# A re-planned order of loads, stores and matmuls in a fused attention and adapter kernel

## The chip, the cores and the metric

The kernel runs on one core of one Trainium2 chip. A core has a matrix engine (PE), a vector engine (DVE), a scalar engine (ACT), a general engine (POOL) that here only issues loads, and a sync engine (SP) that here only issues stores. Sixteen DMA engines move data between the main memory and the on-chip memory (SBUF). PE writes its results to eight banks of a second memory (PSUM). The metric is the device time of one execution in microseconds (us); lower is better. A profile of one execution has a span that is a little shorter than that time.

## The reference

For each of four batches, with N = 6400 rows and C = 256 channels, a 256 x 256 attention matrix is made from k and q, summed over the rows; then it is applied to v. On every row of that result a small mixture of eight adapters is added, of which the two with the largest gates count.

```python
qn = q / (norm(q, axis=1) + 1e-06)          # B, N, C = 4, 6400, 256, fp32
kn = k / (norm(k, axis=1) + 1e-06)
s = kn.transpose(0, 2, 1) @ qn / tau        # 256 x 256 for each batch
a = softmax(s)
x = (v @ a).reshape(B * N, C)               # 25600 x 256
logits = x @ w_gate                         # 8 experts
topk = two largest logits of each row; w = softmax over those two
delta = sum over the two: w * ((x @ A[e]) @ B[e])   # rank 16
return x + delta
```

So q, k and v are read once (3 x 26.2 MB) and the output is written once (26.2 MB). All of q and k of a batch must have arrived before any output row of that batch can be made.

## The kernel before

The kernel is a Python program that first plans and then emits. A small event simulation (`Plan.run`) plays all steps on five engines and a DMA model, and the order in which it starts them becomes the order of the instructions on each engine. Rows are split over 128 partitions; a batch has 50 "columns" of 128 rows. Loads of q and k come in three parts per batch (17, 17, 16 columns), v in five blocks of ten columns, and so does the output.

```python
STORE = {"zl": 1, "bank": 6, "qk": 6, "v": 3, "vT": 4, "y": 7, "gate": 3, "gz": 4, "gzT": 4, "sq": 1, "ssq": 2, "port": 1}
```

These are the numbers of buffers: three for v blocks, four for transposed v blocks, seven for output blocks. The steps that matter:

```python
def do_load(s, what, b, i, c, n):           # POOL issues; fp32 in memory becomes bf16 in SBUF
    if what == "v":
        t, src, c0 = sb(s, "v", (b, i), [P, PC * max(n for _, n in V), C], BF16), v_v, c
    ...
    nc.gpsimd.dma_start(t[:, c - c0:c - c0 + n, :], src[b, :, c:c + n, :])

def do_G(s, b, c):                          # k.T q of one column, and with it k.T k and q.T q
    for ic in range(CC):
        nc.tensor.matmul(acc[ic][:, 0:256], kt[:, j, ic::CC], qt[:, j, :], ...)
    for ic in range(0 if (b, group_of(c), "k") in OFF else CC):
        nc.tensor.matmul(acc[ic][:, 256:384], ...)      # norm of k on PE
    for ic in range(0 if (b, group_of(c), "q") in OFF else CC):
        nc.tensor.matmul(acc[ic][:, 384:512], ...)      # norm of q on PE
```

For the groups of columns in `OFF` the norms are not made on PE: ACT squares the columns (`do_sq`) and DVE adds the squares (`do_add`, `do_red`). After the last G of a batch comes a chain of short steps (`accs`, `n2`, `rsqrt`, `rq_ps`, `s`, `exp`, `aT`, `waA`, `a`) that makes the attention matrix. Each v block then goes through: `T` (transpose on PE), `Te` (copy out), then for a block in `MERGED` `ZL` (gate logits and adapter input in one matmul) and `ZLe`, or for another block `log` and later `Z`; the gates `m1` to `g2` on DVE; `Ze`, `gzT`, `gzTe`; `Y` (v times a, plus the adapter's output) and `Ye`, the copy to the output buffer by ACT or DVE.

```python
def do_Ye(s, b, i, c):
    copy(s, sb(s, "y", (b, i), [P, PC, C], FP32)[:, c:c + 2, :], held["bank", ("Y", b, i, c)])

def do_store(s, b, i, c, n):                # SP issues
    lo = i * PC + c
    nc.sync.dma_start(out_v[b, :, lo:lo + n, :], held["y", (b, i), ""][:, c:c + n, :])
```

A store can be held back until a given load has landed (`HOLD`). This is done by a small copy in SP's queue that reads the end of that load's tile; the store follows it:

```python
def do_hold(s, kind, b, i):
    src = ...                               # 16 elements of the last column of that load
    nc.sync.dma_start(scrap, src)
```

The planner's DMA model serves the load queue and the store queue in proportion to a size of packet, with fixed latencies:

```python
LAT = 0.07
DMA_LAT = 1.8
ISSUE = 0.55
ISSUE_LAT = 1.8
STORE_LAT = 1.4
...
WORDS = ('q10 v00 v01 v02 q11 v03 q12 v04 v10 v11 q20 v12 v13 v14 q21 v20 v21 v22 q22 q30 '
         'q31 q32 v23 v24 v30 v31 v32 v33 v34')       # order of loads after q and k of batch 0
HOLD = {(0, 0): ('k', 3, 1), (0, 1): ('k', 1, 2), (0, 4): ('k', 3, 2), (1, 0): ('k', 3, 1),
        (1, 1): ('k', 3, 2), (1, 2): ('k', 3, 2), (1, 3): ('k', 3, 2), (1, 4): ('k', 3, 2),
        (2, 0): ('k', 3, 1), (2, 1): ('k', 3, 2), (2, 4): ('k', 3, 1)}
```

A word such as q11 stands for part 1 of q and of k of batch 1; v03 is block 3 of v of batch 0. `do_warm` fills idle time of PE with matmuls whose result is not used, so that PE's clock stays up.

Of the kernel before, what the change touches and what calls it, by code (L numbers as in the profile page):

```python
# [18 lines left out]
class Step:  # L19
# [3 lines left out]
    def __init__(self, key, eng, deps, rank, take, give, size=0.0):  # L23
        self.packet = max(size, 0.08)
        self.key, self.eng, self.deps, self.rank = key, eng, deps, rank
        self.take, self.give, self.size = take, give, size
        self.users, self.place = [], {}
        self.ready, self.end, self.on = 0.0, None, None
        self.left = len(deps)
        self.only = next(iter(eng)) if len(eng) == 1 else None  # L30


class Clock:


    WINDOW, FIRST, LOW, HIGH = 3.413, 0.31, 0.5, 0.8
# [32 lines left out]
class Plan:  # L69

    LAT = 0.07
    DMA_LAT = 1.8
    ENGINES = ("PE", "DVE", "ACT", "POOL", "SP")
    ISSUE = 0.55
    ISSUE_LAT = 1.8
    STORE_LAT = 1.4
    OUT = 8

# [15 lines left out]

    def run(self, head):
# [4 lines left out]
        loads, queue, stores = list(self.loads), [], []  # L100
        now, out, left = 0.0, 0, sum(s.key[0] != "warm" for s in self.steps.values())
        free["POOL"] = 0.2
        clock = Clock()

# [5 lines left out]
        def can_take(s):  # L110
            return all((kind, name) in held or self.store[kind] for kind, name in s.take)

        def start(s, eng):
            for kind, name in s.take:
                if (kind, name) not in held:
                    held[kind, name] = self.store[kind].pop(0)
                    s.place[kind] = held[kind, name]
            s.on = eng
            s.t = now
            self.out.append(s)  # L120

# [5 lines left out]
        while left:  # L127
            again = False
            if (loads and free["POOL"] <= now + 1e-9 and out < self.OUT and can_take(loads[0])):
                s = loads.pop(0)  # L130
                start(s, "POOL")
                out += 1
                free["POOL"] = now + self.ISSUE
                push(free["POOL"], "free", None)
                push(now + self.ISSUE_LAT, "asked", s)
                again = True
            for e in self.ENGINES:
# [3 lines left out]
                for s in wait[e]:  # L141
                    if not can_take(s) or (s.key[0] == "warm" and not clock.idle(now)):
                        continue
# [3 lines left out]
                    if best is None or (s.rank, s.seq) < (best.rank, best.seq):  # L147
                        best = s
# [7 lines left out]
                if e == "SP":  # L156
                    push(now + self.STORE_LAT, "store", best)
                else:
                    push(free[e], "end", best)
# [3 lines left out]
            busy = [x for x in (queue, stores) if x]  # L163
            t = events[0][0] if events else float("inf")
            base = max(now, head)

            share = sum(x[0].packet for x in busy)
            if busy:
                t = min(t, base + min(x[0].size / x[0].packet for x in busy) * share)
            assert t < float("inf"), [s.key for s in self.steps.values() if s.end is None][:20]  # L170
            if t > base:
                for x in busy:
                    x[0].size -= (t - base) * x[0].packet / share
                    if x[0].size < 1e-6:
                        push(t + self.DMA_LAT, "landed", x[0])
                        out -= x is queue
                        x.pop(0)
            now = max(now, t)
            while events and events[0][0] <= now + 1e-9:
                _, _, what, s = heapq.heappop(events)  # L180
                if what == "asked":
                    queue.append(s)
                elif what == "store":
                    stores.append(s)
# [3 lines left out]
                elif what == "landed":  # L188
                    push(now + (SAFE if s.on == "POOL" else 0.0), "end", s)
                    for u in s.users:  # L190
                        if u.key[0] == "hold":
                            u.left -= 1
                            if u.left == 0:
                                push(now, "ready", u)
                elif what == "end":
# [6 lines left out]
                    for u in s.users:  # L202
                        u.left -= u.key[0] != "hold"
                        if u.left == 0 and u.eng and u.key[0] != "hold":
                            push(now + (0.0 if s.on == u.only else self.LAT), "ready", u)
# [10 lines left out]
V = ((0, 1), (1, 1), (2, 1), (3, 1), (4, 1))  # L216
# [13 lines left out]

def make_plan(B, order, ahead):
# [6 lines left out]
    for kind, b, i in order:  # L238
        if kind == "v":
            p.add(("load", "v", b, i, V[i][0] * PC, V[i][1] * PC), {}, (), 0, take=(("v", (b, i)),),  # L240
                  size=LOAD * V[i][1] * PC + 0.062)
            continue
        for c, n in PARTS.get((b, i), QK[i:i + 1]):
            for h in "qk":
                p.add(("load", h, b, i, c, n), {}, (), 0, take=(("qk", (h, b, i)),), size=LOAD * n + 0.062)

    for h in "qk":
        p.add(("cast", h), {"ACT": 0.6}, [("load", h, 0, 0) + PARTS[0, 0][0]], 0)
    p.loads[2].size += 0.5
    for b in range(B):  # L250

        for i, (c0, n) in enumerate(QK):
            for c in range(c0, c0 + n):
# [8 lines left out]
                p.add(("G", b, c), {"PE": 0.442 - 0.112 * sum((b, group_of(c), w) in OFF for w in "kq")}, deps,  # L262
# [4 lines left out]
        for w in "kq":  # L267
# [5 lines left out]
            for x, g in enumerate(halves):  # L273
                c, n = GROUPS[g]
                i = max(i for i, q in enumerate(QK) if q[0] <= c)
                p.add(("sq", w, b, g), {"ACT": 0.2 + 0.2125 * n},
                      [k for k in p.steps if k[:4] == ("load", w, b, i) and k[4] < c + n and c < k[4] + k[5]]
                      + [("cast", w)] * ((b, c) == (0, 0)), pos["qk", b, i] - SQ, take=(("ssq", (w, b)) if x == 0 else ("sq", (w, b, g)),),
                      give=(("qk", (w, b, i)),))
                if x:  # L280
                    p.add(("add", w, b, g), {"DVE": 0.15 + 0.268 * n},
# [4 lines left out]
            if halves:  # L286
                p.add(("red", w, b), {"DVE": 1.9}, [before], pos["qk", b, len(QK) - 1] - 1, give=(("ssq", (w, b)),))
                p.add(("n2p", w, b), {"PE": 0.35}, [("red", w, b), ("G", b, NC - 3)], -100, take=(("bank", ("n2p", w, b)),))
                late.append(w)
        if b == 0:  # L290
            p.add(("wts",), {"DVE": 1.8}, [("load", "k", 0, len(QK) - 1) + PARTS[0, len(QK) - 1][1]], -200)
# [3 lines left out]
        p.add(("accs", b, 1), {"ACT": 0.38}, [end], ch)  # L295
        p.add(("n2", b, 0), {"DVE": 0.45}, [end], ch)
        p.add(("accs", b, 0), {"ACT": 0.38}, [("n2", b, 0)], ch)
        p.add(("n2", b, 1), {"DVE": 0.45}, [("accs", b, 1)], ch)
        p.add(("rsqrt", b), {"DVE": 1.9 + 0.2 * len(late)},
              [("n2", b, 0), ("n2", b, 1)] + [("n2p", w, b) for w in late], ch, take=(("port", b),),  # L300
              give=(("port", b),) + tuple(("bank", ("n2p", w, b)) for w in late))
        p.add(("rq_ps", b), {"PE": 0.45}, [("rsqrt", b)], ch, take=(("bank", ("rq", b)),))
        for ic in range(2):
            p.add(("s", b, ic), {"DVE": 0.42}, [("rq_ps", b), ("accs", b, ic)], ch, give=(("bank", ("rq", b)),))
            p.add(("exp", b, ic), {"ACT": 0.68}, [("s", b, ic)], ch)
            p.add(("aT_ps", b, ic), {"PE": 0.14}, [("exp", b, ic)], ch, take=(("bank", ("aT", b)),))
        p.add(("recip", b), {"DVE": 0.17}, [("exp", b, 0), ("exp", b, 1)], ch)
        p.add(("aT", b), {"DVE": 0.42}, [("aT_ps", b, 0), ("aT_ps", b, 1)], ch, give=(("bank", ("aT", b)),))
        p.add(("waA_ps", b), {"PE": 0.35}, [("aT", b), ("wts",)], ch, take=(("bank", ("waA", b)),))
        p.add(("waA", b, 0), {"DVE": 0.35}, [("waA_ps", b), ("recip", b)], ch, give=(("bank", ("waA", b)),))  # L310
# [676 lines left out]
```

## Time and profile before

| what | value |
|---|---|
| device time, median of 3 runs | 254.41 us (254.39 to 254.47) |
| span of the profiled execution | 252.7 us (its device time 254.46) |
| PE busy | 217.8 us, 86% of the span |
| DVE busy | 192.7 us, 76% |
| ACT busy | 151.1 us, 60% |
| mean granted clock of PE | 0.986 of full speed |
| read from and written to main memory | 78.91 MB, 26.21 MB |

The page lists busy time by engine, then the span in 40 slices with one digit each (9 means 90% or more), the DMA queues (q0 carries the loads that POOL issues, q1 what SP issues, q10 what ACT issues), the chain of work that ended last, and the costliest groups of instructions. A group line has the line of the kernel, the engine and the operation, the output and the input with their shapes, the count, the busy time, the mean of one in ns, and the idle time of that engine just before, with what ended it. In the table of stretches, the DMA share is the mean busy share of the sixteen DMA engines; it can be a little above 1 since packets overlap. GB/s there counts the bytes that arrive.

### The profile page before, as it was taken

How to read it: one execution, taken by the hardware profiler on the slowest of the kernel's cores; microseconds unless marked ns; L12 is line 12 of the kernel's file. 1: busy time of each engine (PE TensorE's matmuls, PEld its weight loads, DVE VectorE, ACT ScalarE, POOL GpSimd, SP SyncE). 2: the span in 40 equal slices, each digit the busy share in tenths (PEclk: the TensorE clock that was granted, in tenths of full speed). 3: DMA queues.
4: the chain of work that ended last, by engine and by line, in shares of the span. 5: the costliest groups of instructions: out<-in, count | busy, mean ns of one | idle time of the engine just before them, and what ended most of it. 6: DMA issues, size and time to landing. Idle time of an engine off the chain costs nothing.

```text
span 252.7 us, 5852 instructions
## 1 busy us (share of the span) xinstructions
PE 217.8 (86%) x2357; PEld 193.0 (76%) x2357; DVE 192.7 (76%) x528; ACT 151.1 (60%) x269; POOL 27.1 (11%) x54
## 2 busy tenths in 40 slices
PE   0274995988999998689999999889999979999990
PEld 0162882876999996579899899779999769999980
DVE  0055589869899987588899899489898898889850
ACT  5454427546786543975667768362674846657671
POOL 7003010040002002000500100500000000000000
PEclk9998899999999999999999999999999999999997
DMA  8999999999999999999999999999999999999996
GB/s 251 217 217 209 211 223 208 217 218 215 215 217 241 303 305 298 224 213 221 210 215 220 215 217 217 211 212 313 317 251 353 322 341 317 337 392 415 404 408 249
DMA packets 11243, 66.70 MB, mean 264 GB/s; under 512 B 1360, under 2 KB 1744, under 8 KB 6608
## 3 DMA queue, kind: packets, MB, share of 16 engines
q0 software_dynamic: 6912, 38.80, 74.4%
q1 hardware_dynamic: 3968, 26.87, 26.1%
q10 hardware_dynamic: 336, 0.66, 0.8%
q8 instruction: 18, 0.29, 0.4%
q14 instruction: 9, 0.07, 0.1%
HBM read 78.91 MB, written 26.21 MB: 416 GB/s over the span
## 4 chain that ended last, share of the span: by engine, by line
PE 53%; DMA 32%; issue 5%; DVE 4%; ACT 2%; POOL 1%; POOLq 0%; DVEq 0%
DMA v<-in_v_dram 18%; PE Y_ps L915 13%; PE acc L593 10%; DMA qk<-in_q_dram 10%; PE Y_ps L920 6%; PE T_ps L788 5%; PE ZL_ps L812 5%; DMA qk<-in_k_dram 5%; PE gzT_ps L902 4%; PE acc L597 3%; PE acc L602 2%; PE Z_ps L879 1%; ACT a_exp L715 1%; DVE a_bf L763 1%; PE log_ps L826 1%
## 5 line engine op out<-in xcount | busy, mean ns | idle before, releaser
L593 PE MATMUL acc<-qk 128*128 128x256 bf16 x400 | 69.6, 282 | 17.0 <-DMA qk<-in_k_dram 9.4
L915 PE MATMUL Y_ps<-a_bf,vT 128*128 128x256 bf16 x400 | 60.0, 273 | 0.2 <-DVE acc_sb L710 0.2
L621 DVE TENSOR_TENSOR ssq<-ssq,sq 128x1280 f32<-128x1280 f32 (+1 forms) x27 | 43.4, 1606 | 19.6 <-ACT sq L615 19.6
L769 ACT COPY y<-Y_ps 128x512 f32<-128x512 f32 x79 | 46.2, 586 | 16.6 <-PE Y_ps L920 13.5
L593 PEld LDWEIGHTS <-qk 128*128 128x128 bf16 x400 | 34.2, 101 | 20.7 <-DMA qk<-in_k_dram 11.5
L615 ACT ACTIVATE sq<-qk 128x1280 f32<-128x1280 bf16 (+1 forms) x27 | 36.9, 1368 | 17.7 <-DVE ssq L621 16.6
L915 PEld LDWEIGHTS <-vT 128*128 128x128 bf16 x400 | 38.9, 98 | 4.7 <-issue 0.3
L920 PE MATMUL Y_ps<-ball,gzT 128*128 128x256 bf16 x200 | 38.2, 273 | 0.0
L597 PE MATMUL acc<-qk 128*128 128x128 bf16 x242 | 34.5, 224 | 0.0
L788 PE MATMUL T_ps<-ident,v 128*128 128x128 f32 x200 | 27.6, 274 | 0.6 <-DVE waA_sb L757 0.4
L769 ACT COPY vT<-T_ps 128x512 f32<-128x512 f32 (+1 forms) x44 | 21.2, 510 | 10.9 <-PE T_ps L788 10.5
L597 PEld LDWEIGHTS <-qk 128*128 128x128 bf16 x242 | 24.4, 101 | 3.5
L890 DVE TENSOR_TENSOR gz<-zl,gateg 128x256 bf16<-128x256 f32 x70 | 26.3, 445 | 0.3
L578 POOL DMA_DIRECT2D v<-in_v_dram x20 | 11.5, 576 | 133.7 <-PE T_ps L788 92.8
L788 PEld LDWEIGHTS T_ps<-ident,v 128*128 128x128 f32 x200 | 22.3, 141 | 1.6 <-DVE waA_sb L757 0.6
L602 PE MATMUL acc<-qk 128*128 128x128 bf16 x168 | 23.4, 222 | 0.0
L902 PE MATMUL gzT_ps<-ident,gz 128*128 128x128 f32 x100 | 20.9, 281 | 2.6 <-DVE gateg L868 1.4
L920 PEld LDWEIGHTS <-gzT 128*128 128x128 bf16 x200 | 19.6, 98 | 2.3
L812 PE MATMUL ZL_ps<-waA_sb,vT 128*128 128x136 bf16 x280 | 19.5, 223 | 1.7 <-DVE waA_sb L757 1.5
L771 DVE COPY gzT<-gzT_ps 128x256 f32<-128x256 f32 (+1 forms) x40 | 15.0, 380 | 7.1 <-PE gzT_ps L902 5.6
L812 PEld LDWEIGHTS <-vT 128*128 128x128 bf16 x280 | 17.7, 98 | 2.4 <-issue 2.1
L615 ACT ACTIVATE ssq<-qk 128x1536 f32<-128x1536 bf16 x8 | 11.9, 1489 | 11.4 <-DMA qk<-in_q_dram 7.4
(80 smaller groups left out, 271.3 us busy)
## 6 DMA issues: line engine op xcount, KB each, us to landing
out_dram<-y SPq DMA_DIRECT2D x18, 1280.0 KB, 16.7
v<-in_v_dram POOLq DMA_DIRECT2D x20, 640.0 KB, 20.5
qk<-in_q_dram POOLq DMA_DIRECT2D x7, 1088.0 KB, 23.7
qk<-in_k_dram POOLq DMA_DIRECT2D x7, 1088.0 KB, 28.4
qk<-in_q_dram POOLq DMA_DIRECT2D x4, 512.0 KB, 19.2
qk<-in_k_dram POOLq DMA_DIRECT2D x4, 512.0 KB, 22.5
qk<-in_q_dram POOLq DMA_DIRECT2D x2, 1024.0 KB, 19.4
qk<-in_k_dram POOLq DMA_DIRECT2D x2, 1024.0 KB, 23.8
```

Of the source, the lines that this page charges most:

```text
L593: nc.tensor.matmul(acc[ic][:, 0:256], kt[:, j, ic::CC], qt[:, j, :], start=c == 0, stop=False, skip_group_check=True)
L597: nc.tensor.matmul(acc[ic][:, 256:384], kt[:, j, ic::CC], kt[:, j, ic::CC], start=False, stop=False, skip_group_check=True)
L602: nc.tensor.matmul(acc[ic][:, 384:512], qt[:, j, ic * P:(ic + 1) * P], qt[:, j, ic * P:(ic + 1) * P], start=False, stop=c == NC - 1, skip_ ...
L615: nc.scalar.activation(out[:, 0:n, :], t[:, j:j + n, :], ACT.Square)
L621: nc.vector.tensor_tensor(out=t, in0=t, in1=held["sq", (w, b, g), ""][:, 0:n, :], op=OP.add)
L769: nc.scalar.copy(out, in_)
L788: nc.tensor.matmul(ps[:, j, :], vt[:, c + j, :].bitcast(FP32), W["ident32"], is_transpose=True, start=(j == 0), stop=(j == n - 1))
L812: nc.tensor.matmul(ps[:, j, :], vT_of(b, i, c + j)[:, :, ic], st[b]["waA"][:, ic, :], start=(j == 0 and ic == 0), stop=(j == n - 1 and ic ...
L890: nc.vector.tensor_tensor(out=pairs[:, h].rearrange("p c (e r) -> p c e r", e=E), in0=z[:, 2 * h:2 * h + 2, :].rearrange("p c (e r) -> p c ...
L902: nc.tensor.matmul(ps[:, j, :], pairs[:, j * P:(j + 1) * P], W["ident32"], is_transpose=True, start=(j == 0), stop=(j == n // 2 - 1))
L915: nc.tensor.matmul(ps[:, j, :], vT_of(b, i, c + j)[:, :, ic], st[b]["a"][:, ic, :], start=(j == 0 and ic == 0), stop=False, skip_group_che ...
L920: nc.tensor.matmul(ps[:, j, :], pair[:, :, j], W["B"], start=False, stop=(j == 1), skip_group_check=True)
```

## The change

The planner gets a new DMA model: each DMA engine's stream of rows is played one by one, the two queues take turns row by row, and a row of n columns takes a time from n. The durations of the steps are set to measured ones, each engine's results get a tail before others may use them, and the allowance SAFE for loads goes from 0.5 to 0. With that model a new load order, new holds, new sets OFF and MERGED were searched, in a replay that also tries drops of the clock and late loads. In the program itself two things change: a held store now waits on the load's own semaphore and the `hold` copies are gone; and the output buffers and the v buffers are each one tile, of which blocks use slices.

```diff
-    LAT = 0.07
-    DMA_LAT = 1.8
+    TAIL = {"PE": 0.164, "DVE": 0.083, "ACT": 0.1}
+    LAT = 0.037
-    ISSUE = 0.55
-    ISSUE_LAT = 1.8
-    STORE_LAT = 1.4
+    ISSUE, ISSUE_LAT = 0.52, 1.8
+    STORE, STORE_LAT = 0.46, 0.85
     OUT = 8
+    PIPE, FETCH = 2.9, 1.005
+    ROW, SEM = (0.003, 0.012), (0.021, 0.006)
+    DMA_LAT, SPREAD, SKEW = 0.31, 0.6, 0.008
...
+        def fill():
+            nonlocal turn, ahead
+            while ahead < self.PIPE and (rings[0] or rings[1]):
+                turn = 1 - turn if rings[1 - turn] else turn
+                s = rings[turn][0]
+                if s.rows:
+                    s.rows -= 1
+                    us, last = s.size * self.FETCH + self.ROW[turn], None
...
-                p.add(("Ye", b, i, c0), {"ACT": 0.6, "DVE": 0.7}, [("Y", b, i, c0)], x - .9,
-                          take=(("y", (b, i)),), give=(("bank", ("Y", b, i, c0)),))
+                p.add(("Ye", b, i, c0), {"ACT": 0.482, "DVE": 0.6}, [("Y", b, i, c0)], x - .9,
+                          take=(("y", pieces(b, i)),), give=(("bank", ("Y", b, i, c0)),))
...
-WORDS = ('q10 v00 v01 v02 q11 v03 q12 v04 v10 v11 q20 v12 v13 v14 q21 v20 v21 v22 q22 q30 '
-         'q31 q32 v23 v24 v30 v31 v32 v33 v34')
-HEAD = 2.6
-LOAD = 0.304
+WORDS = ('v00 q10 q11 q12 v01 v02 q20 v03 v04 q21 v10 q22 v11 v12 v13 q30 v14 v20 v21 q31 v22 q32 v23 v24 v30 '
+         'v31 v32 v33 v34')
+HEAD = 5.05
+COL = 1.024 * 1.17647 / 32
 WARM = 150
-AHEAD = 2.7
+AHEAD = 4.7
-HOLD = {(0, 0): ('k', 3, 1), (0, 1): ('k', 1, 2), (0, 4): ('k', 3, 2), (1, 0): ('k', 3, 1),
-        (1, 1): ('k', 3, 2), (1, 2): ('k', 3, 2), (1, 3): ('k', 3, 2), (1, 4): ('k', 3, 2),
-        (2, 0): ('k', 3, 1), (2, 1): ('k', 3, 2), (2, 4): ('k', 3, 1)}
+HOLD = {(0, 0): ('v', 2, 3), (0, 1): ('v', 2, 4), (0, 2): ('v', 3, 4), (0, 3): ('v', 3, 3), (0, 4): ('v', 0,
+        0), (1, 0): ('v', 3, 3), (1, 1): ('v', 2, 4), (1, 2): ('v', 2, 4), (2, 0): ('v', 1, 4), (3, 1):
+        ('v', 0, 0), (3, 3): ('v', 1, 0)}
...      (OFF: 35 groups become 37; MERGED: 14 blocks become 12; SQ 2 -> 5; PARTS of the first load (0, 2) -> (0, 4))
-SAFE = 0.5
+SAFE = 0
...
+    Y = sbuf.tile([P, STORE["y"] * PC, C], FP32, name="y")
+    VS = sbuf.tile([P, STORE["v"] * PC, C], BF16, name="v")
...
-    def do_hold(s, kind, b, i):
-        ...
-        nc.sync.dma_start(scrap, src)
...
     def do_store(s, b, i, c, n):
         lo = i * PC + c
-        nc.sync.dma_start(out_v[b, :, lo:lo + n, :], held["y", (b, i), ""][:, c:c + n, :])
+        at_y = at["y", (b, i)] * PC + c
+        p = 0
+        for rows in SHARES if (b, i) in SPLIT else (P,):     # SPLIT is empty: one transfer
+            r = nc.sync.dma_start(out_v[b, p:p + rows, lo:lo + n, :], Y[p:p + rows, at_y:at_y + n, :])
+            if (b, i) in HOLD and not p:
+                tc.add_manual_dep(r.ins, loaded[held_by(plan, b, i)],
+                                  mybir.DependencyInfo(mybir.DependencyClass.Sync, mybir.DependencyReason.DATA),
+                                  reason="held")
+            p += rows
```

The first four columns of q and k of batch 0 come by SP and ACT as before; only their place in the plan's tables has changed.

## The prediction

> **What bounds the kernel now.** I read three views: the page (DMA row of the slices, DMA queues, HBM total), then a table of busy time by stretch, and last the waits of the store queue. First the page:
>
> ```profile
> DMA  8999999999999999999999999999999999999996
> q0 software_dynamic: 6912, 38.80, 74.4%
> q1 hardware_dynamic: 3968, 26.87, 26.1%
> q10 hardware_dynamic: 336, 0.66, 0.8%
> HBM read 78.91 MB, written 26.21 MB: 416 GB/s over the span
> ```
>
> The reader is to see that the DMA engines are never idle for a slice: only the first (8) and last (6) are below 9. Queue shares add to 74.4 + 26.1 + 0.8 + 0.5 (instructions) = 101.8% of the span (packets overlap a little, so over 100% is possible). No engine is as full: PE has 86%, of which 39 matmuls (10.4 us) only keep its clock up. The stretches:
>
> ```profile
> 0.00:10.00 10.00, 1.89 (x8) 1.04 (x8) 0.52 (x4) 3.58 (x4) 5.06 (x14) 1.00 0.93 236
> 10.00:37.00 27.00, 19.27 (x173) 15.60 (x174) 14.60 (x17) 13.78 (x10) 3.71 (x7) 0.94 1.04 215
> 37.00:77.00 40.00, 35.31 (x362) 29.35 (x360) 34.83 (x95) 26.24 (x46) 3.94 (x6) 1.00 1.04 215
> 77.00:105.00 28.00, 24.91 (x283) 22.39 (x281) 21.99 (x66) 14.80 (x28) 3.76 (x8) 1.00 1.04 283
> 105.00:167.00 62.00, 59.82 (x652) 54.58 (x650) 52.95 (x136) 42.48 (x76) 8.48 (x16) 1.00 1.03 215
> 167.00:224.00 57.00, 53.82 (x645) 49.28 (x643) 50.44 (x157) 33.43 (x72) 2.12 (x4) 1.00 1.04 314
> 224.00:238.00 14.00, 14.00 (x169) 13.12 (x167) 12.47 (x42) 10.03 (x22) 0.00 (x0) 1.00 1.01 424
> 238.00:247.00 9.00, 8.77 (x85) 7.63 (x82) 4.91 (x14) 6.40 (x14) 0.00 (x0) 1.00 0.96 394
> 247.00:250.00 3.00, 0.00 (x0) 0.00 (x0) 0.00 (x0) 0.39 (x1) 0.00 (x0) 0.86 0.96 383
> 250.00:252.70 2.70, 0.00 (x0) 0.00 (x0) 0.00 (x0) 0.00 (x0) 0.00 (x0) 0.50 0.15 58
> ```
>
> Columns: stretch, its length, PE, weight load, DVE, ACT, POOL busy, clock, DMA share, GB/s. GB/s counts what lands in SBUF; a load turns fp32 into bf16, so 215 means 430 GB/s read. From 10 to 224 us the share stands at 1.03 to 1.04 whatever PE does. I take 1.04 as "full". All DMA work is 1.018 x 252.7 = 257.2 us of share, or 257.2 / 1.04 = **247.4 us at full pace**. A check by bytes: 78.91 + 26.21 = 105.12 MB at 430 GB/s is 244.5 us. So the span is 5.3 us above its DMA work: first 10 us 10 x (1.04 - 0.93) / 1.04 = 1.1; 224 to 238, 0.4; 238 to 247, 0.7; 247 to 250, 0.2; the end, 2.3; rounding of the shares is the rest.
>
> PE is a close second: from 37 to 247 us it is busy 196.6 of 210 us, and the end of the chain of waits is PE matmul after PE matmul until 246.8, one ACT copy of 0.59, then the last store (issued 247.4). Both limits meet within 5 us.
>
> ```profile
> SPq L928 <- DVE y L771: 111.6, 6, 73.0
> SPq L645 <- DMA qk<-in_k_dram: 88.7, 3, 76.7
> SPq L645 <- DMA scrap<-qk: 3.1, 1, 3.1
> ```
>
> This is the store queue. L645 is the "hold" copy: SP waits for a k load, then copies 32 bytes of it to scrap, and stores wait for that copy's landing (4.9 us median from issue). These waits are intended: they keep stores out of the loads' way.
>
> **What the Trainium skill says.** "DMA: Bandwidth & Descriptors", section "Queues, rings and completion order": a DMA engine takes turns between the queues that have work, packet by packet. The trace agrees: from 170 to 180 us, with both queues full, 317 GB/s land. If stores move s and loads land l (reading 2l), s + l = 317 and s + 2l = 423 (423 is the pace near there, an estimate from the 424 of the store stretch) give l = 106, s = 211: read side equal to store side, equal turns. The new planner models these turns. Section "Anatomy of one DMA": DMA engines don't wait on semaphores, the issuing sequencer does. L645's 88.7 us on SP agree. So putting the load's semaphore on the store itself costs nothing new. "TensorE: Matmul & The Clock Gate", section "What's actually happening": an idle PE falls to half clock. Granted clock 0.94 from 10 to 37 us agrees, and shows little is left to save.
>
> **The change, part by part.**
>
> (1) The hold steps go; the store waits on the load itself. Removed: 3 copies of 0.51 to 0.60 us on SP and 3 round trips of about 5 us. A store may start some 5 us sooner after its load. But the DMA share around 167 and 183 us is 1.04 without it, so another transfer only moves behind: 0 us. The packets removed are 32-byte ones: under 0.1 us.
>
> (2) One tile Y and one tile VS in place of slots with tags. Same bytes, same slots (7 and 3); 0 us, provided overlaps are tracked by region. They are for the qk tiles: PE worked on the first four columns of one from 6.5 to 8.4 us, while the load of its other 13 landed only at 13.9.
>
> (3) OFF and MERGED. Counting the columns of the listed groups: 195 columns have their sum of squares off PE before, 205 after. A column is two 128-wide matmuls; the chain shows two 256-wide in 0.22 us, so 0.11 us a column: PE -1.1 us. ACT gets 10 more columns at 1275 ns / 5 = 0.26 (its group of squares, 128x1280 form): +2.6; DVE adds them up at 1487 / 5 = 0.30: +3.0. Merged blocks fall from 14 to 12: per block a ZL of 1.18 becomes log 0.48 plus Z 1.12 on PE, +0.42, so +0.8; four zl copies of about 0.47 go: -3.8 on ACT and DVE. Net: PE -0.3, ACT plus DVE +2. All off the DMA path.
>
> (4) Order of loads and of stores: the real change. A column (128 x 256 fp32 = 131 kB) at 430 GB/s takes 0.305 us, a block of ten 3.05. Loads on the software queue start near 5 us, with 8 columns already on other queues. Before, 530 columns stand ahead of and including q,k of (3,2), with three stores (77 to 105 us) between. After, 530 too, but the holds let only store (0,4) out early: (0,0) to (0,3) and (1,0) to (1,2) wait for v (2,3) or later. So q,k (3,2) land at 5 + 522 x 0.305 + 3.05 = 167 us (before: about 183, the hold on it issues at 182.96), v (2,3) at 170. Then six v loads and 19 stores are left: 250 columns, 76 us, and the data end at 246.5 if DMA never idles. Loads and stores take turns, so the last v lands at about 170 + 6 x 6.1 = 207 us (before: the software queue's last packet starts at 224.3).
>
> Does PE keep up? Between 42 us (first a ready, an estimate) and 170 it has G of three batches, 150 x 0.44 - 164 x 0.11 = 48; eight whole blocks at about 6.3 (T 1.09, ZL 1.18, gzT 0.55, Y 5 x 0.66, or 0.42 more unmerged) = 50; first halves of four more, 10; chains, 9. That is 117 of 128 us. After 170: 15 for those four, 50 for eight blocks, 3 for the last chain: PE ends near 240 plus a few waits, ahead of the DMA end. So stores stay queued to the end and the 0.4 + 0.7 + 0.2 us can be won, and about 1.2 of the last 2.3 (the last completion remains): **at most 2.5 us**. Span 252.7 - 2.5 = 250.2; the timed figure is 1.8 above the span (254.46 against 252.7), so 252.0 at best.
>
> (5) Measured durations for the planner, SAFE 0, another AHEAD: no instruction costs less; they only make the order match the chip. I give the plan two thirds of the possible 2.5: 254.41 - 1.6 = **252.8 us**.
>
> **The rivals.**
>
> (a) PE starves for y slots. All seven are held until v (2,3) lands, so block (1,3) has nowhere to write from about 130 to 170 us, and only T and gate work of four blocks (four vT slots) fills the hole. I counted 11 us spare in that stretch; PE needs about 6 us of slack at the end. Should G of batch 3 or a chain fall late as well, PE ends at 248 or more: 255 to 257 us. For it: PE already idles under 4% from 105 to 167. Against it: the holds were searched with a model that knows the slots.
>
> (b) Transfers already hidden: DMA is full in both, only order moves, the tail keeps its shape (last block in three pieces in both): 254 to 254.6 us. For it: FINE and UNITS don't change.
>
> (c) ACT or DVE becomes the bound through SAFE 0 and tighter times. DVE has 76%; +3 us makes 78%. In-order engines that were planned too tightly wait for late loads; worth +1 to +3 us, little seen now.
>
> (d) More than 2.5 us: it would need fewer DMA bytes or a faster pace; nothing in the change does that.
>
> **Range and chances.** Floor 252.0, which a slightly faster pace with fewer mixed stretches could stretch to 251; the centre 252.8; (b) at 254.4; (a) and (c) up to 257. Eight in ten: 251.0 to 256.5. Faster by 2% means below 249.3, under the DMA floor: 0.03. Slower by 2% means above 259.5, which needs a DMA hole of 6 us: 0.04. Within 2%: 0.93.
>
> **What would show it.** Right: no L645 on the store queue; DMA share 1.03 or more from 10 us to nearly the end; one store before 165 us; last v landed by 212; PE's last matmul before 244, with stores queued behind it at 420 GB/s or more. Wrong: a DMA share below 1 in any stretch from 120 to 240 us, Y matmuls or L769 and L771 copies waiting for out_dram stores (rival a), a clock below 0.97, or PE ending at 247 again (b).

## The result, and the profile after

| | before | after |
|---|---|---|
| device time, median | 254.41 us | 257.53 us (256.77 to 257.83) |
| ratio to before | | 1.0118, 95% interval 1.0095 to 1.0141 |
| span of the profiled execution | 252.7 us | 255.0 us (its device time 256.77) |
| mean granted clock of PE | 0.986 | 0.951 |
| PE, DVE, ACT busy | 217.8, 192.7, 151.1 us | 220.3, 171.3, 164.1 us |

The kernel became slower by 1.2%, where the prediction had 252.8 us (251.0 to 256.5), a gain. The page of the kernel after, with the rows that answer to those shown of before:

```profile
DMA  8999999999999999999999999999999999999996
GB/s 247 216 218 210 213 222 213 217 215 216 208 223 217 209 219 214 216 213 264 271 213 211 221 216 208 216 215 325 427 416 279 322 262 304 242 419 435 420 416 254
...
q0 software_dynamic: 6912, 38.80, 74.3%
q1 hardware_dynamic: 3872, 26.87, 26.1%
...
HBM read 78.91 MB, written 26.21 MB: 412 GB/s over the span
```

The bytes are the same, the row of digits is the same, and the queues' shares are the same within 0.1%. By the busy share of the whole span nothing has happened to the DMA engines. Only the rate over the span fell, from 416 to 412 GB/s, because the span grew. The stretches of after (stretch, length, PE, weight load, DVE, ACT and POOL busy, clock, DMA share, GB/s landed):

```profile
77.00:105.00 28.00, 27.11 (x312) 24.51 (x311) 26.71 (x89) 22.27 (x45) 2.64 (x5) 1.00 1.04 215
105.00:167.00 62.00, 61.05 (x698) 55.58 (x696) 54.11 (x144) 46.53 (x89) 7.93 (x15) 1.00 1.04 225
167.00:224.00 57.00, 51.19 (x586) 47.90 (x583) 40.83 (x141) 38.00 (x86) 2.64 (x5) 0.94 1.02 315
224.00:238.00 14.00, 14.00 (x160) 13.05 (x159) 7.31 (x30) 12.32 (x29) 0.00 (x0) 1.00 1.01 422
238.00:247.00 9.00, 9.00 (x94) 8.28 (x93) 2.32 (x6) 7.45 (x16) 0.00 (x0) 1.00 1.00 422
247.00:250.00 3.00, 0.31 (x3) 0.03 (x1) 0.00 (x0) 0.86 (x2) 0.00 (x0) 1.00 1.03 417
250.00:255.00 5.00, 0.00 (x0) 0.00 (x0) 0.00 (x0) 0.00 (x0) 0.00 (x0) 0.53 0.52 209
```

Two things stand out. From 238 to 250 us the stores are now dense (422 and 417 GB/s; before 394 and 383): the small gaps that the prediction wanted closed are closed. But the span is longer, so the bytes must have been lost earlier. And in 167 to 224 PE was busy 51.2 of 57 us at a clock of 0.94 (before 53.8 at 1.00). The wait that belongs to it is in the waits of after (engine, what it wanted, the releaser: total, times, longest):

```profile
ACT y L810 <- DMA out_dram<-y: 8.4, 1, 8.4
...
PE n2p_ps L685 <- ACT y L810: 5.8, 1, 5.8
```

and in its chain of waits (start, length, what):

```profile
147.71 25.75 DMA v<-in_v_dram
...
173.47 6.65 DMA out_dram<-y
...
180.14 0.59 ACT y L810
...
180.78 1.87 PE n2p_ps L685 x8
```

All seven output buffers are full. The store of block (0,0) waits until v (2,3) has landed at 173.5 us and takes 6.65 us; only then does an ACT copy find an output buffer, and PE, whose next step needs ACT, stands for 5.8 us. Its granted clock is 0.50 from 180 to 184 us. This is rival (a) of the prediction, to the letter, so it was the first suspect.

**Where the time is lost, counted in bytes.** I summed what DMA moved up to each moment (a packet counts in full when it begins; a load counts twice its landed bytes, since it reads fp32 and writes bf16) and compared it with the kernel before; the difference divided by 430 GB/s is how far after lies behind. At 190 us it is 0.02 us behind, at 220 us 2.78 us. So the whole loss falls into 30 us, and it begins ten microseconds after PE's stand has ended. The stretch of 190 to 222 us, first before, then after:

```profile
190.00:222.00 32.00, 29.71 (x359) 26.89 (x358) 28.01 (x102) 19.24 (x47) 2.12 (x4) 1.00 1.03 334
```

```profile
190.00:222.00 32.00, 32.00 (x396) 30.27 (x396) 24.71 (x95) 26.91 (x64) 2.45 (x5) 1.00 1.02 284
```

PE is busier than before (32.0 of 32 us, at full clock). The DMA share is 1.02 against 1.03. Yet 284 GB/s land in place of 334. (A different mix of loads and stores changes landed GB/s too; the 2.78 us above are free of that, as loads are counted by what they read.) The Trainium skill, "Perfetto Trace Analysis", section "Identifying the Most-Contended Engine", says to judge DMA by its throughput against the memory's peak and not by occupancy, which misleads with sixteen engines; these two lines agree with it.

A busy share that stays while bytes fall means that packets last longer. Two neighbouring stretches of after, in both of which only stores move:

```profile
190.00:192.00 2.00, 2.00 (x37) 1.90 (x37) 2.00 (x7) 1.89 (x7) 0.34 (x1) 1.00 1.03 420
192.00:194.00 2.00, 2.00 (x28) 1.81 (x25) 2.00 (x8) 1.49 (x4) 0.00 (x0) 1.00 1.00 297
```

In the packets of the trace, the rows of stores (10 KB) that begin from 192 to 194 us take 551 ns on the mean (up to 756), where the same kernel has 385 to 398 at full pace; rows of loads (5 KB landed) that begin from 217 to 220 us take 553 (up to 1.8 us), where it has 399. The row time above full pace in 190 to 222 us comes to an estimated 2.4 to 2.8 us for each DMA engine, which is nearly the whole loss; the rest is idle time. The long rows come in bursts, near 192 to 194, 201 to 202 and 217 to 220 us, where one queue had run empty or nearly so. They are not simply what a transfer alone in line looks like: from 208 to 210 us only loads move, and their rows take 399 to 401 ns.

So what was queued? POOL's timeline of after (start, length, what, and in brackets the idle time before and its releaser) shows few loads:

```profile
159.07 0.53 POOL L627 DMA_DIRECT2D v<-in_v_dram  x1 [10.83 <-PE T_ps L828]
189.81 0.53 POOL L627 DMA_DIRECT2D v<-in_v_dram  x1 [30.21 <-PE gzT_ps L942]
199.65 0.53 POOL L627 DMA_DIRECT2D v<-in_v_dram  x1 [9.31 <-PE T_ps L828]
201.93 0.53 POOL L627 DMA_DIRECT2D v<-in_v_dram  x1 [1.75 <-PE T_ps L828]
```

But before had hardly more:

```profile
162.85 1.62 POOL L578 DMA_DIRECT2D v<-in_v_dram  x3
191.55 0.54 POOL L578 DMA_DIRECT2D v<-in_v_dram  x1 [27.08 <-DMA v<-in_v_dram]
199.87 0.53 POOL L578 DMA_DIRECT2D v<-in_v_dram  x1 [7.78 <-PE T_ps L788]
```

In both, v loads come one by one from 190 us on, whenever a v buffer comes free. What differs is the store queue. At 190 us six stores are issued and not landed in before, two in after. The store queue's waits of after, now on the store instruction itself:

```profile
SPq L971 <- DVE y L812: 122.4, 3, 111.9
SPq L971 <- DMA v<-in_v_dram: 68.5, 4, 58.2
```

Three blocks that are finished and could be stored, (0,2), (0,3) and (1,0), some 9 us of DMA work, are held until v (3,3) and v (3,4) have landed, at about 219 and 225 us. So from 190 us on DMA has only what PE has just made, plus single loads. Of the 32 us, the store queue is empty for 6.7 us (never in before) and the load queue for 6.9 us (2.2 in before).

To compare runs I count the **reserve**: the DMA time of all transfers that have been issued and taken up, but have not begun (worked out from issues and packets of a trace; an estimate). Before: mean 15.0 us in 190 to 222 us, never below 1.5 us. After: mean 3.5 us, and below 1.5 us for 6.1 of the 32 us. The means are firm within some 0.8 us; the time below 1.5 us depends on how long a transfer is taken to need from its issue until it counts (with the shortest times seen in after, 1.65 us for a load and 0.84 for a store, it is 2.7 us).

This gives two theories that can be told apart. **Theory S** (shallow queue): the three blocks held to v (3,3) and (3,4) are missing from the store queue, and that starves DMA after 190 us. **Theory P** (PE's stand): PE's stand and half clock at 175 to 186 us set the end. The runs below state what each expects.

### The profile page after: what moved, and what is told of

It is laid out like the page before. It is cut to its first block, busy times and chain, and to the rows that moved or that the text cites. A ratio compares the mean times of both kernels' runs of the same rounds, so it can differ in the third digit from the quotient of the medians.

```text
span 255.0 us, 5808 instructions
## 1 busy us (share of the span) xinstructions
PE 220.3 (86%) x2361; PEld 195.8 (77%) x2361; DVE 171.3 (67%) x487; ACT 164.1 (64%) x308; POOL 26.2 (10%) x54
## 4 chain that ended last, share of the span: by engine, by line
PE 44%; DMA 27%; DVE 19%; ACT 6%; issue 2%; DVEq 0%; POOLq 0%
DMA v<-in_v_dram 21%; PE Y_ps L955 12%; DVE ssq L670 9%; PE Y_ps L960 6%; PE T_ps L828 6%; PE ZL_ps L852 4%; PE gzT_ps L942 4%; PE acc L642 4%; DMA qk<-in_q_dram 3%; DMA out_dram<-y 3%; DVE ssq L676 3%; ACT sq L664 3%; PE Z_ps L919 2%; DVE gz L930 2%; PE n2p_ps L685 2%
## 5 line engine op out<-in xcount | busy, mean ns | idle before, releaser
L642 PE MATMUL acc<-qk 128*128 128x256 bf16 x400 | 73.7, 288 | 12.1 <-ACT qk L815 6.5
L670 DVE TENSOR_TENSOR ssq<-ssq,sq 128x1280 f32<-128x1280 f32 (+1 forms) x29 | 46.6, 1608 | 32.0 <-ACT ssq L664 22.8
L810 ACT COPY y<-Y_ps 128x512 f32<-128x512 f32 x87 | 50.9, 589 | 18.2 <-DMA out_dram<-y 8.4
L664 ACT ACTIVATE sq<-qk 128x1280 f32<-128x1280 bf16 (+1 forms) x29 | 39.6, 1367 | 24.0 <-DVE ssq L670 13.7
L642 PEld LDWEIGHTS <-qk 128*128 128x128 bf16 x400 | 35.9, 104 | 15.6 <-DMA qk<-in_k_dram 6.6
L955 PEld LDWEIGHTS <-vT 128*128 128x128 bf16 x400 | 38.7, 98 | 4.2
L627 POOL DMA_DIRECT2D v<-in_v_dram x20 | 10.6, 532 | 135.5 <-PE T_ps L828 90.5
L930 DVE TENSOR_TENSOR gz<-zl,gateg 128x256 bf16<-128x256 f32 x60 | 22.7, 446 | 0.2
L651 PEld LDWEIGHTS <-qk 128*128 128x128 bf16 x220 | 21.0, 103 | 2.0
L664 ACT ACTIVATE ssq<-qk 128x1536 f32<-128x1536 bf16 (+1 forms) x8 | 11.7, 1458 | 14.4 <-DMA qk<-in_k_dram 10.2
L646 PEld LDWEIGHTS <-qk 128*128 128x128 bf16 x170 | 17.7, 104 | 2.9
L810 ACT COPY zl<-ZL_ps 128x408 f32<-128x408 f32 (+1 forms) x38 | 15.5, 466 | 5.8 <-PE ZL_ps L852 5.3
L852 PE MATMUL ZL_ps<-waA_sb,vT 128*128 128x136 bf16 x240 | 17.9, 231 | 1.1 <-ACT vT L810 1.1
```

The lines of the kernel that those rows point to most:

```text
L646: nc.tensor.matmul(acc[ic][:, 256:384], kt[:, j, ic::CC], kt[:, j, ic::CC], start=False, stop=False, skip_group_check=True)
L651: nc.tensor.matmul(acc[ic][:, 384:512], qt[:, j, ic * P:(ic + 1) * P], qt[:, j, ic * P:(ic + 1) * P], start=False, stop=c == NC - 1, skip_ ...
L664: nc.scalar.activation(out[:, 0:n, :], t[:, j:j + n, :], ACT.Square)
L670: nc.vector.tensor_tensor(out=t, in0=t, in1=held["sq", (w, b, g), ""][:, 0:n, :], op=OP.add)
L810: nc.scalar.copy(out, in_)
L852: nc.tensor.matmul(ps[:, j, :], vT_of(b, i, c + j)[:, :, ic], st[b]["waA"][:, ic, :], start=(j == 0 and ic == 0), stop=(j == n - 1 and ic ...
```

## The experiments

HOLD is also an input of the planner, so an edit of it can change the order of the instructions too. In the traces of e4 and e8 the order on PE, DVE, ACT and POOL is that of before. In e1 and e6 it is that of after until 210 us, in e7 that of e3 until 207 us. In e3 it leaves that of after at 138 us, and in e2 at 75 us: these two change more than a hold.

The runs, in one table. "Behind" is at 220 us, relative to before, as above; the reserve is for 190 to 222 us, its mean and the time below 1.5 us.

| run | median us | ratio [95% interval] | behind, us | reserve: mean, time below 1.5 us |
|---|---|---|---|---|
| before | 254.4 | | 0 | 15.0, 0 |
| after | 257.53 | 1.0118 [1.0095, 1.0141] | 2.78 | 3.5, 6.1 |
| e1_release | 254.67 | 1.0012 [1.0005, 1.0019] | 0.43 | 10.6, 0 |
| e2_shallow | 254.53 | 1.0018 [0.9995, 1.0041] | 0.37 | 4.2, 3.7 |
| e3_drop10 | 254.44 | 1.0002 [0.9994, 1.0011] | -0.10 | 12.5, 0 |
| e4_old_nohold | 254.50 | 1.0003 [0.9994, 1.0012] | 0.02 | not counted |
| e5_again | 256.66 | 1.0092 [1.0076, 1.0108] | 2.83 | 3.5, 6.2 |
| e6_one | 254.93 | 1.0018 [1.0012, 1.0025] | 0.67 | 6.2, 0 |
| e7_nostand | 255.77 | 1.0052 [1.0037, 1.0068] | 1.72 | 4.5, 3.1 |
| e8_old_late | 258.31 | 1.0147 [1.0131, 1.0164] | 4.05 | 3.5, 6.5 |
| e9_fine0 | 254.58 | 1.0005 [0.9997, 1.0013] | -0.21 | 12.3, 0 |
| e10_pairs | 254.16 | 0.9986 [0.9980, 0.9993] | -0.69 | 9.6, 0 |

### e1: let the three blocks go earlier

```diff
-HOLD = {..., (0, 2): ('v', 3, 4), (0, 3): ('v', 3, 3), ..., (1, 0): ('v', 3, 3), ...}
+HOLD = {..., (0, 2): ('v', 2, 4), (0, 3): ('v', 2, 4), ..., (1, 0): ('v', 2, 4), ...}
```

> Only the hold of three stores is moved: blocks (0,2), (0,3) and (1,0) wait for v (2,4), landed at 176 us, and not for v (3,4) and (3,3), landed at 225 and 219. PE still stands from 175 to 181 us, since the seven output buffers are still all held until v (2,3). Theory S (shallow DMA queues: after 190 us the three held stores, 9 us of DMA work, are missing from the store queue, and DMA runs at 375 to 392 GB/s of source bytes for 30 us in place of 422): 254.3 to 255.2 us, with the bytes moved by 220 us within 0.5 us of the kernel before. Theory P (PE's stand for an output buffer and the low clock after it set the end): 257 to 258 us, as in the changed kernel.

Measured: 254.67 us; of the 3.1 us lost 2.9 are back. The stand of PE is still there (5.1 us for the same step), and so is the low clock; two stretches of e1:

```profile
182.00:190.00 8.00, 8.00 (x61) 7.04 (x62) 5.14 (x24) 5.29 (x13) 0.00 (x0) 0.69 1.00 422
190.00:222.00 32.00, 32.00 (x386) 30.02 (x384) 23.81 (x87) 26.50 (x62) 2.64 (x5) 1.00 1.03 337
```

In 182 to 190 us the granted clock is 0.69 (in after it was 0.79). DMA nevertheless lands 337 GB/s in the stretch in which after landed 284. The first four v loads from 159 us on are issued at 159.5, 190.4, 200.3 and 202.5 us, 0.4 to 0.6 us later than after's. So what changed for DMA is when the three stores could start. At 210 us, up to which the order of instructions on the other engines is that of after, e1 is 0.33 us behind and after 1.69. Theory S is borne out; theory P, which says that the stand itself costs the time, is not. A second, smaller hole opens late: no store is issued between 227.1 and 237.8 us, as PE is late with block (3,1), and at 240 us e1 is 1.02 us behind. At the end 0.25 us are left of it.

### e2: other late holds, without the stand

```diff
-HOLD = {(0, 0): ('v', 2, 3), ..., (0, 3): ('v', 3, 3), ..., (2, 0): ('v', 1, 4), ...}
+HOLD = {                     ..., (0, 3): ('v', 3, 4), ..., (2, 0): ('v', 3, 4), ..., (1, 4): ('v', 2, 3)}
```

> The reverse of the first: block (0,0) is not held, so an output buffer comes free before 170 us and PE need not stand; but (0,3) and (2,0) are held until v (3,4), beside (0,2), so that three or four finished blocks are kept from the store queue until the end of the loads. Theory S: 257 to 258.5 us, DMA again 2 to 3 us behind the kernel before at 220 us, although PE doesn't stand. Theory P: 254 to 255 us.

Measured: 254.53 us, with one execution at 257.78 (so the interval is wide). The reserve did come out low, 4.2 us on the mean and 3.7 us below 1.5 us, but the loss at 220 us is 0.37 us only. This is a miss for theory S as I had put it in numbers: a low reserve is not enough for a loss. Nor is an empty queue: e2's load queue is empty for 15.4 of the 32 us and its store queue for 5.9. In e2's trace, when one queue was empty, the other mostly held two transfers or more (loads were issued in pairs near 195 to 197 and 205 to 206 us, four stores stood in line at 188 us), where in after it often held one. That is a description after the fact, and not tested; and since e2 has another order of instructions from 75 us on, more than the holds differs.

### e3: one block not held at all, and no stand

```diff
-HOLD = {..., (1, 0): ('v', 3, 3), ...}
+HOLD = {...}                                    # (1, 0) goes when it is made
```

> Only the hold of block (1,0) is taken off. Both the stand of PE and the shallow queues should go, as one more buffer turns over early and PE runs ahead. Both theories: 253.8 to 254.8 us, PE's last matmul near 243 us. If it stays at 257, both are wrong, and the cause lies in what all variants share: the new steps' order, the one-tile buffers, or the wait on the load itself.

Measured: 254.44 us, the same as before. One store of (1,0) before the wait for v (2,3) frees an output buffer, PE doesn't stand, and the reserve is 12.5 us, although (0,2) and (0,3) are held to the same loads as in after (they leave at 219.3 and 212.3 us). Block (1,3) leaves at 154.9 us, in after at 182.3. Stretches of e3:

```profile
190.00:222.00 32.00, 31.58 (x390) 29.06 (x388) 26.49 (x106) 24.74 (x61) 1.58 (x3) 1.00 1.03 339
...
238.00:247.00 9.00, 4.35 (x40) 3.66 (x38) 0.29 (x1) 4.38 (x8) 0.00 (x0) 1.00 1.00 418
```

PE's last matmul ends at 242.35 us, 4.4 us earlier than the 246.8 of before, and stores are queued behind it at 418 GB/s. This is the picture that the prediction had drawn, its sign "PE's last matmul before 244" included, and still the time is that of before. How the end of e3 looks, microsecond by microsecond:

```profile
247.00:248.00 1.00, 0.00 (x0) 0.00 (x0) 0.00 (x0) 0.00 (x0) 0.00 (x0) 0.73 0.93 369
248.00:249.00 1.00, 0.00 (x0) 0.00 (x0) 0.00 (x0) 0.00 (x0) 0.00 (x0) 0.50 0.75 301
249.00:250.00 1.00, 0.00 (x0) 0.00 (x0) 0.00 (x0) 0.00 (x0) 0.00 (x0) 0.50 0.60 238
250.00:251.00 1.00, 0.00 (x0) 0.00 (x0) 0.00 (x0) 0.00 (x0) 0.00 (x0) 0.50 0.22 84
251.00:252.00 1.00, 0.00 (x0) 0.00 (x0) 0.00 (x0) 0.00 (x0) 0.00 (x0) 0.50 0.04 16
```

The share doesn't drop at once, it tapers, which fits DMA engines that end at different times; the last packet ends at 251.4. The shares add to 2.54, so if each engine is busy until its end, the mean engine ends at 247 + 2.54 = 249.5 us. In before the same sum is 3.28, the mean engine ends at 250.3, and the last one at 251.6. The denser end of e3 thus gained 0.7 us for the mean engine, but 0.2 us for the last, and the run ends with the last one. No run with these transfers has a median below 254.4 us; that this is a floor for them was not tested.

### e4: the old order, stores waiting on the loads themselves

```diff
     def do_hold(s, kind, b, i):
+        return
...
         r = nc.sync.dma_start(out_v[b, :, lo:lo + n, :], ...)
+        if (b, i) in HOLD:
+            tc.add_manual_dep(r.ins, loaded[HOLD[b, i]], ..., reason="held")
```

> The kernel before, in its own order, with only the emission of the hold changed: no copy to scrap, the store waits on the load's semaphore. My step (1): no effect, 254.2 to 254.6 us. A theory in which the direct wait is what costs: 256 us or more.

Measured: 254.50 us, ratio 1.0003 with 1 inside the interval: no cost and no gain of the replaced wait shows.

### e5: the kernel after once more

No edit.

> The changed kernel itself once more, for the spread of its times and a second trace. If the loss between 190 and 222 us is the shallow queue, every execution loses there, by different amounts: 256.5 to 258 us, DMA 2 to 3.5 us behind the kernel before at 220 us in this trace too. If it was an accident of the first trace, the two traces lose in different places.

Measured: 256.66 us (256.34 to 257.36), 0.9 us below the first time, with overlapping intervals; 2.83 us behind at 220 us, with the bytes missing in the same places (near 192, 200 and 217 us). The loss belongs to the kernel, not to one execution.

### e6: only one of the three goes earlier

```diff
-HOLD = {..., (1, 0): ('v', 3, 3), ...}
+HOLD = {..., (1, 0): ('v', 2, 4), ...}
```

> One of the three late holds is moved: (1,0) waits for v (2,4); (0,3) and (0,2) still wait for v (3,3) and (3,4). One block more, 3 us, is then waiting behind what DMA does from 190 us on. Theory S, with the loss growing steeply as the reserve falls under about 3 us: 254.6 to 255.5 us. A theory in which each block held costs in proportion: 257.5 - 2.9 / 3 = 256.5 us.

Measured: 254.93 us. One released block (3 us of DMA work) takes the reserve from 3.5 to 6.2 us and the loss from 2.78 to 0.67 us. The reserve is never below 1.5 us. The stores are not worth the same each: the first one brings most. Of the three late holds two are still there.

### e7: late holds without the stand, in the new order

```diff
-HOLD = {(0, 0): ('v', 2, 3), (0, 1): ('v', 2, 4), ..., (1, 0): ('v', 3, 3), (1, 1): ('v', 2, 4), ...}
+HOLD = {(0, 0): ('v', 3, 4), (0, 1): ('v', 3, 4), ...,                      (1, 1): ('v', 3, 4), ...}
```

> No hold on (1,0), so PE doesn't stand; but (0,0), (0,1), (0,2), (1,1) all wait for v (3,4) and (0,3) for v (3,3), which brings the reserve of DMA work from 190 to 222 us down to that of the changed kernel. Theory S: 255.5 to 258 us. Theory P: 254.4 us. If 254.4 as in the second experiment, a small reserve alone isn't enough, and PE's stand or what follows from it must come with it.

Measured: 255.77 us, 1.3 us above e3, from which it differs in three later holds and, from 207 us on, in the order of instructions; at 210 us it is already 0.69 us behind, e3 0.15 ahead. PE does not stand for an output buffer here, so a loss of this kind needs no stand.

### e8: late holds alone, in the old kernel

```diff
-HOLD = {..., (0, 4): ('k', 3, 2), ..., (1, 1): ('k', 3, 2), (1, 2): ('k', 3, 2), (1, 3): ('k', 3, 2), ...}
+HOLD = {..., (0, 4): ('v', 3, 3), ..., (1, 1): ('v', 3, 3), (1, 2): ('v', 3, 4), (1, 3): ('v', 3, 4), ...}
```

(Built on before, with its copies to scrap.)

> The kernel before, with its own planner and order, but four of its stores held later: (0,4) and (1,1) until v (3,3), (1,2) and (1,3) until v (3,4), in place of k of batch 3. PE doesn't stand and its clock stays up. Theory S: the reserve from 190 to 222 us falls from 15 to 3 us and the time goes to 256 to 258.5 us, by a loss in that stretch. If holds alone do no harm: 254.4 to 254.8 us.

Measured: 258.31 us, 3.9 us above before. The order of instructions on PE, DVE, ACT and POOL is that of before; only the store queue differs. In it the four stores come behind both late holds, so that all four are issued from 224.4 us on, and block (2,4) stands behind the hold on v (3,3), but it is ready only at 220.1 us, after that hold has let go. The stretch of e8:

```profile
190.00:222.00 32.00, 29.70 (x359) 26.84 (x358) 27.99 (x103) 19.57 (x47) 2.12 (x4) 1.00 0.95 278
```

PE, DVE and ACT did the same work in it as before (29.70 against 29.71 us of PE), so they felt nothing of it. Only DMA lacked work: 278 GB/s, and here even the share falls, to 0.95. The load queue is empty for 1.3 us only, the store queue for 5.6. With e1 this shows the cause from both sides: taking the late holds out of the new kernel returns the time, putting such holds into the old one takes it.

### e9: a coarser end

```diff
-HOLD = {..., (1, 0): ('v', 3, 3), ...}          # as in e3
-FINE = 2
+FINE = 0
```

> The third experiment (no hold on (1,0), 254.44 us) with the last two blocks stored whole and not in three pieces each. PE ended near 242.5 us there, so there is slack for a later last store, and DMA, the bound, has fewer and longer rows at its end. If DMA's work alone sets the time: 254.0 to 254.3 us. If the last store's latency after PE counts: 254.4 us or more.

Measured: 254.58 us, e3 being 254.44. How finely the last blocks are cut makes no difference that shows.

### e10: fewer and longer rows, with holds that leave a reserve

```diff
+PAIRS = {(0, 0), (0, 2), (1, 0), (2, 3), (3, 1)}    # two blocks leave in one store
+HOLD = {(0, 0): ('v', 2, 3), (0, 2): ('v', 3, 1), (1, 2): ('v', 2, 4), (2, 0): ('v', 3, 0), (3, 1): ('v', 0, 0),
+        (3, 3): ('v', 1, 0), (2, 3): ('v', 3, 1), (2, 2): ('v', 3, 1), (2, 4): ('v', 3, 0)}
-FINE = 2
+FINE = 0                                            # and the last part of q, k of batch 3 in one transfer each
```

> As before it, and five pairs of neighbouring blocks are stored by one transfer of twenty columns each, q and k of (3,2) come in one part, and the holds are chosen so that at least 4 us of DMA work wait at nearly all times between 60 and 235 us. The bytes are the same; the stores have 17 transfers fewer rows' starts. If a row's fixed cost is what keeps DMA under its pace: 253.0 to 253.8 us. If only bytes count: 254.2 to 254.4 us.

The number of transfers saved that is named there was too high: there are 15 stores in place of 24. The page of e10:

```profile
DMA packets 9562, 66.70 MB, mean 264 GB/s; under 512 B 1088, under 2 KB 1472, under 8 KB 5056
...
q0 software_dynamic: 6624, 38.80, 74.3%
q1 hardware_dynamic: 2576, 26.87, 25.7%
```

Measured: 254.16 us, 0.9986 of before with an interval below 1, just under the forecast for "only bytes count" and far from the other. It is the fastest of all, by 0.3 us; which of its changes brings that was not separated. There are 15% fewer packets (9562 against 11243), and at 240 us DMA is 1.16 us ahead of before (0.95 if a packet counts as it goes: e10's are longer); at 250 us only 0.23 us are left. In between, the stretches show where it goes:

```profile
238.00:247.00 9.00, 6.47 (x60) 5.61 (x57) 2.92 (x9) 6.25 (x12) 0.00 (x0) 1.00 0.93 394
247.00:255.00 8.00, 0.00 (x0) 0.00 (x0) 0.00 (x0) 0.00 (x0) 0.00 (x0) 0.55 0.31 129
```

DMA runs out of stores (share 0.93): the last two are issued at 241.3 and 245.1 us, when PE and the copies have made their blocks (PE's last matmul ends at 244.5 us). Being ahead is worth nothing while DMA waits for these.

Not tried: an eighth output buffer, which would go to the root of PE's stand.

## Why the prediction was wrong, step by step

**(1) and (2), the waits of the stores and the single tiles: right at 0 us.** e4 has (1) alone (1.0003 [0.9994, 1.0012]); e3 has (1), (2), (3) and most of (4), at 1.0002. One reading in (1) was off: stores did not wait some 5 us for the copy's landing. In before a store is issued 0.6 to 0.9 us after the copy (166.88 and 167.45, 182.96 and 183.81 us).

**(3), OFF and MERGED: harmless, as said; PE's size was off for another reason.** PE is busy 220.3 us in after, +2.5, where -0.3 was expected. In e3, with the same OFF and MERGED and no stand, it is 217.8, as before, so the 2.5 us go with the stand and the low clock after it. (Both new kernels have 23 matmuls that only keep the clock up, before had 39, so the sizes of the other steps were not checked one by one.) DVE fell by 21 us and ACT rose by 13, because the plan moved copies from DVE to ACT (of y, gzT and zl); the expectation of +2 for both together missed this shift, but neither engine sets the time.

**(4) failed, at the sentence "Then six v loads and 19 stores are left: 250 columns, 76 us, and the data end at 246.5 if DMA never idles".** Up to there the arithmetic was 3.4 us too early: q,k of (3,2) landed at 170.4 us (167 predicted), v (2,3) at 173.5 (170). The 76 us are right as a sum of work. What failed is the condition. It took the 19 stores as a stock that lies ready at 170 us, from which DMA draws at will; "So stores stay queued to the end" was concluded from PE's total work. But four of them came free with v (2,3) and (2,4), three were locked until about 219 and 225 us, and the rest had still to be made by PE, which made none while all output buffers were full. The prediction read the holds for what they keep away before 170 us and for the output buffers that they fill (its rival (a)), and never for what is left in line when they let go. The term that was missing is the 2.8 us of DMA work not moved between 190 and 220 us; e1 returns most of it, e8 makes it.

A second error has another cause. The last v landed at 225.1 us, where "about 207" had assumed that loads queue without gaps; in fact they wait for v buffers (the 30.2 us on POOL's timeline), in before as well (27.1 us, the last v at 224.6). PE ended at 247.3 in place of 240.

**The gain of "at most 2.5 us" did not exist either.** It was the shortfall of the share against 1.04 in the last 30 us, and a part of the drain. e3 fills 238 to 247 us (418 GB/s, before 394) and ends where before ended. Two things in the traces speak to that. Where stores alone run densely they move 418 to 425 GB/s at a share of 1.00 to 1.01 (before, after and e3 in 224 to 238, after and e3 in 238 to 247 us), so 1.04 belongs to stretches with loads, and the 0.4 us counted for 224 to 238 was not there. And of the 0.7 us that e3 wins in the mean of the engines the last one wins 0.2: a mean share is no measure of the end. In after the 3.4 us by which v (2,3) was late had used up the gain already: with 76 us of work behind it the data would have ended at 249.7 us, not 246.5, even without a hole.

**The rivals.** (a), at 255 to 257 us, came nearest in time, and its mechanism took place, but PE's end was not what cost the time: e1 keeps the stand (5.1 us) and half clock and lies 0.3 us above before; e7 and e8 lose 1.3 and 3.9 us without it. Yet the stand had its part in after: while PE stood no block was made, (1,3) left 27 us later than in e3, and e3, with two of the three late holds and no stand, loses nothing. What starved DMA in after is both together, a stock of finished blocks that was locked and another that was not yet made; releasing the first (e1) or making the second earlier (e3) is enough. (b), that nothing changes, is what e3 and e9 show. (c) did not happen: DVE is busy 67% in after.

**The signs.** Of the signs of being right, "no L645" and "one store before 165 us" (issued at 114.8) came true; a share of 1.03 or more (1.02 in 167 to 224 us), the last v by 212 us (225.1) and PE's last matmul before 244 (247.3) did not. Of the signs of being wrong, "a clock below 0.97" (0.951), the wait of the copies for out_dram and PE's end at 247 came true. The sign meant to show a starved DMA, "a share below 1 in any stretch from 120 to 240 us", does not show in the stretches of the table (1.02 at 284 GB/s in 190 to 222); in stretches of 2 us it shows here and there (0.83 from 202 to 204 us), but not where the rows were long (1.00 at 297 GB/s).

**What stays open.** Why e2, with a reserve nearly as low as after's and e7's, loses so little, and why rows last longer in bursts. A low reserve was present in each run that lost over 1 us (after, e5, e7, e8), and in no run without it was more than 0.7 us lost; but the mean of the reserve doesn't set the size of the loss: after and e8, both at 3.5 us, are 2.8 and 4.1 us behind, e2 at 4.2 and e7 at 4.5 are 0.4 and 1.7. If one counts with the shortest times from issue until a transfer counts, the time with a reserve below 1 us is 0.2 (e2), 0.4 (e7), 1.5 (after) and 3.4 us (e8), in the order of the losses; but e2 and e7 lie too close for that to explain them.

## What to carry to other kernels

A hold on a store has two ends: ask not only what it keeps out of the way, but whether DMA still has issued work in line until the hold lets go; here a reserve of some 10 us on the mean cost 0.3 us at most (e1, e10), 6 us cost 0.5 us (e6), and 3.5 to 4.5 us cost from nothing clear of noise (e2) to 3.9 us (e8). Count DMA progress in bytes moved (by source bytes for a load that converts), against the run before, moment by moment: that showed the place of the loss, where the busy share of whole stages showed none. And an engine's visible stand, with a dropped clock, is not yet the cause; a run that keeps the stand and removes the other suspect decides.

## What the runs showed of the hardware that was not expected

- A busy DMA share can hide a loss of pace: in after, with stores alone, it is 1.03 at 420 GB/s from 190 to 192 us and 1.00 at 297 GB/s from 192 to 194. Store rows of 10 KB that take 385 to 398 ns at full pace took up to 756 there, load rows with 399 ns up to 1.8 us near 217 to 220 us, in bursts where a queue had run empty or nearly so; loads that moved alone (208 to 210 us) kept 399 to 401 ns.
- The sixteen DMA engines drift apart. In after the completions of one load lie 1.0 us apart at 10 us and from 173.90 to 176.51 us, 2.6 us, for v (2,4); in before a load that landed at 197.6 us has them 6.2 us apart, and later ones 0.8 to 2.3. The last one sets when a load counts as landed.
- Some five microseconds of PE standing, plus its half clock after, cost 0.3 us in a kernel whose PE is busy 86% of the time (e1).
